# Another written order for the head of a fused memory-attention and spatial-gating kernel

## The chip, the cores and the metric

The kernel runs on one core of a Trainium2 chip. The metric is the device time of one execution in microseconds, the median of several runs. Engines are named as the profile names them: PE is TensorE (PEld its weight loads), DVE VectorE, ACT ScalarE, POOL GpSimd, SP SyncE, which here only issues DMAs.

## What is computed

For each of 8 batches, attention over 32 learned memories in 8 heads, then a gated feed-forward layer that mixes along the sequence:

```python
a = softmax(phi, axis=2)                      # (8, 8, 576, 32)
k_m = einsum('bhsm,bhsd->bhmd', a, k); v_m = einsum('bhsm,bhsd->bhmd', a, v)
attn = softmax(q @ k_m.T / sqrt(64)) @ v_m    # (8, 8, 576, 64)
x = attn.transpose(0, 2, 1, 3).reshape(8, 576, 512)
h = relu(x @ w_in)                            # w_in 512 x 1024
u, v = h[..., :512], h[..., 512:]
v_n = (v - mean(v)) / sqrt(var(v) + 1e-6)
v_s = einsum('ts,bsd->btd', w_spatial, v_n) + b_spatial[None, :, None]
return (u * v_s) @ w_out
```

w_in and w_out arrive as 64-bit floats, so they are decoded on the chip; everything else is 32 bits wide.

## The kernel before

The work is cut into small generator functions; a *step* runs one of them up to its next `yield`, which issues a handful of instructions. There is no scheduler: the order in which steps are taken is the order of the instructions on every engine's queue and on SP's DMA queue, and each engine works through its queue in that order, waiting at an instruction until what it needs is there. The steps of weights and of the first batch (the head) are listed by hand in the string `START`; from the second batch on, `PLAN` gives the order of one batch's steps, taken again for each batch:

```python
for kind, n, ahead in tokens(START):
    step(kind, n, ahead)
for b in range(1, B):
    for at, (kind, n, ahead) in enumerate(steps):
        ...
```

A token is a letter, a block number, a prime for each batch that it works ahead, and `*n` for n steps of it. The letters are:

- P (`memory_weights`): load phi, its maximum over the rows (`mx`, L319 to L325), transposes `mt` and `mb`, the subtraction L349, exp L356, row sums `es`.
- K (`memories`): load k and v, the many small `kvm` matmuls L375 and L387, `den`, then kT and vT.
- Q, S (`queries`, `scores`): q transposed (`tq` by TensorE for the first batch, L478 on VectorE later); scores `sc`, transposed by VectorE (L503), then softmax (maximum L509, subtraction L512, exp L514, sum L517, L519, L520, product L522), transposed back (L533 to L538), split in two parts `ah` (ACT L542) and `al` (DVE L544).
- D, E, L (`load_win`, `decode_win`): w_in's blocks loaded (L178) and decoded: exponent L187, mantissa L193, ACT L205 and L208, DVE L210, the addition L218 (or POOL L216), the product L223 (or POOL L226). X (`prepare_out`) does the same for the four blocks of w_out (`raw_out`, two buffers) and splits each into `woh` and `wol` (L251). The set `ON_VECTOR` says which of the additions, products and splits VectorE does; the rest are GpSimd's.
- W, T, B: load w_spatial and its bias (L260 to L263), transpose it by TensorE (`wt`), split into `wth` and `wtl` (DVE L166 or TensorE L159 with ACT L164); bias row `ws` (POOL L310).
- M (`products`): `mp`, w_in's products with vT, split into `mh` and `ml`.
- V (`gate`): `pv`, relu, statistics (DVE L621, L623), POOL scalars L626 to L631, normalisation on ACT, split into `vh` and `vl` (L641); the fifth block of 64 rows ends in `t` (ACT L645, DVE L649). U (`units`): `pu`, copied to `u` (ACT L672).
- G (`spatial`): `ps`, 28 matmuls per block, the last four with `t` and `ws`; then `g` (L712), `gh` (ACT L723), `gl` (DVE L725). O (`project`): `po` in two halves, the second of which needs blocks 2 and 3 of `gh` and `gl`; then out.

The banks of PSUM are 4 single ones (pool `ps1`) and 2 pairs (`ps2`, for `wt`, `pu` and `ps`).

Of the kernel before, what the change touches and what calls it, by code (L numbers as in the profile page):

```python
# [23 lines left out]


START = """
    P D1 P*3 D0 P*3 D0 P D1 P E0 W L0 E0 D0 E0 T2 L0 P E0 P E0 T2 E0 W P*2 L0 T2*2 P W L0 D0 L1
    L0 E0 T2 E0 L1 W T2*2 L1 K W L1 T4 L1 L0*2 P T1 L1 T4 K L1 T1 Q K D1 T1 D1 T1 K B T1 K T4 K
    Q*2 L0 Q E1 T1 Q P' K Q K Q K E1 L1 T1 Q T4 K E1 K' Q K P' Q P'*2 E1 Q*2 K T0 E1 S E1 P' S T0
    P' T0 S T4 S P' T4 M0 S E1 S T0*3 P' M0*2 X1 P' T0 M0 S*2 P' K' S*2 Q' S*2 T3 E1 T3 P' S P'  # L30
    T3 M0 M1 T3 P'*2 X0 M1 M0 M1 M0 P' M1 Q' M1 S K' S*2 T3 S K' X0 X1 T4 T3 M1 T3 M1 S*2 U1 X1*2
    X0 X1 X0 U0 V1 X0 V1 K' X0 U0 X1 V1 K'*2 X0 V0 U1 Q' K'' P'' V1 V0*2 K' V3 Q' V0 U0 V2 V1 X0
    V1 X1*2 X0 U1 X1 V1 V0 U2 V3 V0 U2 V2 U3 Q' X1 K' U3 K' V4 V3 K' V0 X1 Q' V3 U3 G0 B U2 V4 G1
    V2 K' X0 V4 G0 S'*2 V2 S'*3 G1 V3 M1' P'' X2 M0' P'' X0 V2 V4 V3 V2*2 G1 X3 V4 G0 V4 V3 X2*2
    V4 M0' V4 M1' P'' M1' M0' P'' X2 G1 M0' G1 X2 G0 X3 G2 X2 X3 G2 M1' M0' G0 G1 G0 X2 M0' G2*2
    M1' X2 G1 X3 G3 S' G3 S' P'' X3 G0 G3 X3*2 G0*2 G1*2 P'' G3 G2 S' P'' M1' X2*2 M0' O1 X3 M1'
    X3 G2 G3 O3 S' G3*2 G2 S' G2 X2 X3 O2 K'' O0 S' X3 S' O3 Q'' S' O2 S' G2 S' O3 S'*2 O2 O1 O3
    P''*2 G3 S'*2 P'' O0 O2 P''*2 O1*2 P''*2 G3 O0*2
"""

PLAN = """
# [792 lines left out]
```

## Time and profile before

| | |
|---|---|
| median of 3 runs | 427.18 us (427.04 to 427.68) |
| profiled execution | 425.99 us, of which the span is 424.2 us |
| busy in the span | PE 393.2, PEld 331.6, DVE 299.8, ACT 236.0, POOL 78.9 us |
| granted clock of TensorE | 0.995 on the mean |
| moved by DMA | 50.69 MB |

The span is the time from the first to the last instruction of the profile; the rest of the execution's time lies around it. Busy times of TensorE run from one matmul's start to its modelled end, so pipelined matmuls overlap, and the time from one row's start to the next's is shorter than the duration printed.

### The profile page before, as it was taken

Reading aid. Unit: us, or ns where it says so; the run is one execution under the profiler, and the core shown is the slowest. Engines: PE = TensorE matmul, PEld = TensorE weight load, DVE = VectorE, ACT = ScalarE, POOL = GpSimd, SP = SyncE. Lnnn points to the kernel's source line nnn. Section 1 sums busy time; section 2 is a strip of 40 time slices with the busy share of each in tenths; the row PEclk is TensorE's granted clock in tenths of the full one; section 3 lists DMA queues with packets and bytes.
Section 4 is the critical chain, followed back from the end, with each engine's and each line's share of the span. In section 5 each row is a group of like instructions: output and inputs, shape, how many; then the busy total and the mean of one; then the engine's idle time right before and its main releaser. Section 6 shows DMA issues by size and latency. Waiting matters only on the chain.

```text
span 424.2 us, 9280 instructions
## 1 busy us (share of the span) xinstructions
PE 393.2 (93%) x3828; PEld 331.6 (78%) x3828; DVE 299.8 (71%) x560; ACT 236.0 (56%) x446; POOL 78.9 (19%) x154
## 2 busy tenths in 40 slices
PE   0295998999999999999999999999999999999995
PEld 0172786968988897978888897979798888889884
DVE  1899998995999458955897568946996568834420
ACT  1677787737753376346743575436734476248321
POOL 1345056621200022022200121002100120003100
PEclk9999899999999999999999999999999999999999
DMA  7989935507840948073922659063914500020003
GB/s 287 377 320 289 169 133 181 87 26 132 216 122 16 162 161 181 2 90 109 215 79 55 126 171 168 1 131 109 195 59 69 113 2 2 2 99 2 0 26 99
DMA packets 85790, 50.69 MB, mean 119 GB/s; under 512 B 66226, under 2 KB 70322, under 8 KB 85748
## 3 DMA queue, kind: packets, MB, share of 16 engines
q1 hardware_dynamic: 85748, 50.10, 47.9%
q8 instruction: 30, 0.49, 0.5%
q14 instruction: 12, 0.10, 0.1%
HBM read 40.65 MB, written 9.44 MB: 118 GB/s over the span
## 4 chain that ended last, share of the span: by engine, by line
PE 75%; DVE 13%; DMA 5%; ACT 4%; issue 1%; POOL 1%; SPq 0%; POOLq 0%; DVEq 0%; ACTq 0%
PE ps L701 24%; PE po L741 20%; PE pu L663 11%; PE pv L597 9%; DMA raw<-in_moe_w_in_dram 4%; PE kvm L375 4%; PE mp L565 3%; PE sc L492 2%; DVE power L210 1%; DVE win_sb L218 1%; DVE gl L725 1%; DMA out_dram<-o 1%; DVE st L621 1%; DVE sm L512 1%; PE pv L607 1%
## 5 line engine op out<-in xcount | busy, mean ns | idle before, releaser
L701 PE MATMUL ps<-wth,vh 128*128 128x288 f32 x256 | 57.0, 304 | 0.7 <-ACT u L672 0.4
L626 POOL TENSOR_SCALAR rs<-mv 128x1 f32<-128x1 f32 (+1 forms) x40 | 9.6, 241 | 249.8 <-DVE mv L623 247.2
L723 ACT CAST gh<-g 128x512 fp32r<-128x512 f32 x32 | 19.8, 620 | 63.8 <-DVE g L712 63.8
L701 PE MATMUL ps<-wth,vl 128*128 128x288 f32 x256 | 55.0, 296 | 0.0
L701 PE MATMUL ps<-wtl,vh 128*128 128x288 f32 x256 | 54.5, 294 | 0.0
L741 PE MATMUL po<-woh,gl 128*128 128x512 f32 x128 | 50.9, 398 | 0.8 <-DVE gl L725 0.8
L741 PE MATMUL po<-woh,gh 128*128 128x512 f32 x128 | 50.5, 395 | 0.0
L701 PEld LDWEIGHTS ps<-wth,vh 128*128 128x128 f32 x256 | 41.0, 188 | 12.1 <-ACT mh L574 5.0
L741 PE MATMUL po<-wol,gh 128*128 128x512 f32 x128 | 50.3, 393 | 0.0
L747 ACT COPY o<-po 128x512 f32<-128x512 f32 x36 | 20.9, 586 | 44.1 <-PE po L741 27.5
L701 PEld LDWEIGHTS ps<-wth,vl 128*128 128x128 f32 x256 | 41.0, 188 | 0.3 <-DVE vl L641 0.3
L701 PEld LDWEIGHTS ps<-wtl,vh 128*128 128x128 f32 x256 | 41.0, 188 | 0.0
L636 ACT ACTIVATE vr<-vr,sh,rs 128x512 f32<-128x512 f32 (+1 forms) x40 | 32.6, 814 | 10.2 <-POOL sh L631 9.9
L621 DVE BATCH_NORM_STATS2 st<-vr 128x6 f32<-128x512 f32 (+1 forms) x40 | 27.4, 686 | 12.1 <-ACT vr L602 11.6
L712 DVE TENSOR_TENSOR g<-u,ps 128x576 f32<-128x576 f32 x32 | 23.4, 751 | 12.5 <-PE ps L701 12.5
L741 PEld LDWEIGHTS po<-woh,gl 128*128 128x128 f32 x128 | 24.0, 188 | 8.2 <-DVE gl L725 2.8
L544 DVE TENSOR_TENSOR al<-aT,ah 128x576 fp32r<-128x576 f32 x16 | 12.1, 754 | 24.5 <-ACT ah L542 24.5
L663 PE MATMUL pu<-ah,mh 128*128 128x288 f32 x128 | 28.6, 305 | 0.0
L741 PEld LDWEIGHTS po<-wol,gh 128*128 128x128 f32 x128 | 24.0, 188 | 4.8
L741 PEld LDWEIGHTS po<-woh,gh 128*128 128x128 f32 x128 | 24.1, 188 | 4.6
L663 PE MATMUL pu<-ah,ml 128*128 128x288 f32 x128 | 27.3, 294 | 0.0
L663 PE MATMUL pu<-al,mh 128*128 128x288 f32 x128 | 27.2, 293 | 0.0
(158 smaller groups left out, 893.2 us busy)
## 6 DMA issues: line engine op xcount, KB each, us to landing
kv_sb<-in_k_dram SPq DMA_DIRECT2D x8, 1152.0 KB, 8.1
kv_sb<-in_v_dram SPq DMA_DIRECT2D x8, 1152.0 KB, 9.6
out_dram<-o SPq DMA_DIRECT2D x32, 256.0 KB, 2.4
q_sb<-in_q_dram SPq DMA_DIRECT2D x28, 288.0 KB, 6.2
phi_sb<-in_phi_dram SPq DMA_DIRECT2D x8, 576.0 KB, 4.0
raw<-in_moe_w_in_dram SPq DMA_DIRECT2D x8, 512.0 KB, 7.9
raw_out<-in_moe_w_out_dram SPq DMA_DIRECT2D x4, 512.0 KB, 5.4
w_sb<-in_moe_w_spatial_dram SPq DMA_DIRECT2D x1, 1152.0 KB, 10.8
```

What stands on the lines that cost most here:

```text
L375: nc.tensor.matmul(kvm[r][32 * j : 32 * j + 32], phi_sb[halves[r], j, i, :], kv_sb[halves[r], j, :, i * D : (i + 1) * D], start=(i == 0), ...
L544: nc.vector.tensor_tensor(al[:, r], aT[:, r], ah[:, r, 0:S].bitcast(F32), op=ALU.subtract)
L565: nc.tensor.matmul(mps[r][32 * j : 32 * j + 32, :], vT[D * r : D * r + D, 32 * j : 32 * j + 32], win_sb[D * r : D * r + D, j, cs], start=True,
L597: nc.tensor.matmul(pv, x[:, r, cs], m[:, r, DM:DFF], start=(n == 0), stop=(n == 5))
L621: nc.vector.bn_stats(st6, vr)
L636: nc.scalar.activation(vr, vr, AF.Identity, bias=sh, scale=rs)
L663: nc.tensor.matmul(pu[:, hf, 0:HALF], m[:, r, cs], a[:, r, hf * HALF : (hf + 1) * HALF], start=(n == 0), stop=(n == 5),)
L701: nc.tensor.matmul(ps[:, hf, 0:HALF], a, w[:, hf * HALF : (hf + 1) * HALF], start=(n == 0), stop=(n == len(ops) - 1),)
L712: nc.vector.tensor_tensor(g.rearrange("p (a s) -> p a s", a=2), u[:, dt, :].rearrange("p (a s) -> p a s", a=2), ps[:, :, 0:HALF], op=ALU.mult,
L723: nc.scalar.copy(hi, x)
L741: nc.tensor.matmul(po, a, w, start=(n == 0), stop=(n == 11))
L747: nc.scalar.copy(o, po)
```

## The change

Only the string `START` is another one: the same 382 steps, each kind as often as before, in another sequence. `PLAN`, `ON_VECTOR` and all functions stay. Its first lines, before and after:

```diff
 START = """
-    P D1 P*3 D0 P*3 D0 P D1 P E0 W L0 E0 D0 E0 T2 L0 P E0 P E0 T2 E0 W P*2 L0 T2*2 P W L0 D0 L1
+    P*5 W P D1 P T1 W P*2 D1 P D0 P E0 D0 L0 D0 T2 T1 E0 L0 T1 E0 L0 E0 D0 W T1 L1 K T2 L0 L1 T2
...
 """
```

The order on SP's queue at the start of the program, the loads of phi, w_in (`raw`), w_spatial (`w_sb`, `w_rem`) and its bias (`b_sb`); before:

```order
L330 DMA phi_sb<-in_phi_dram 128x4x288
L178 DMA raw<-in_moe_w_in_dram 128x1024 x4
L260 DMA w_sb<-in_moe_w_spatial_dram 128x4x576
L261 DMA w_rem<-in_moe_w_spatial_dram 64x576
L263 DMA b_sb<-in_moe_b_spatial_dram 1x576 x2
L178 DMA raw<-in_moe_w_in_dram 128x1024 x2
```

and after:

```order
L330 DMA phi_sb<-in_phi_dram 128x4x288
L260 DMA w_sb<-in_moe_w_spatial_dram 128x4x576
L261 DMA w_rem<-in_moe_w_spatial_dram 64x576
L263 DMA b_sb<-in_moe_b_spatial_dram 1x576 x2
L178 DMA raw<-in_moe_w_in_dram 128x1024 x6
```

w_spatial has moved ahead of four loads of w_in; the six loads of w_in now stand together behind it.

On VectorE, from the statistics of the fifth block of V (64 rows) to L649, which gives `t`; before:

```order
L623 BN_AGGR mv<-st_792 64x2
L503 STREAM_TRANSPOSE sm<-sc_0_0_802 128x288
L503 STREAM_TRANSPOSE sm<-sc_0_1_803 128x288
L503 STREAM_TRANSPOSE sm<-sc_1_0_804 128x288
L503 STREAM_TRANSPOSE sm<-sc_1_1_805 128x288
L319 TENSOR_TENSOR half<-phi_sb 128x512
L321 TENSOR_TENSOR half<-half 128x4x64
L641 TENSOR_TENSOR vl<-vr,vh 128x512 x2
L187 TENSOR_SCALAR power<-raw_out 128x512
L193 TENSOR_SCALAR raw_out<-raw_out 128x512
L649 TENSOR_TENSOR t_608<-vr,t_608 64x512
```

and after, with the two transposes that now stand ahead of the statistics:

```order
L187 TENSOR_SCALAR power<-raw_out 128x512
L503 STREAM_TRANSPOSE sm<-sc_0_0_800 128x288
L193 TENSOR_SCALAR raw_out<-raw_out 128x512
L503 STREAM_TRANSPOSE sm<-sc_0_1_801 128x288
L621 BN_STATS st_856<-vr 64x6
L623 BN_AGGR mv<-st_856 64x2
L503 STREAM_TRANSPOSE sm<-sc_1_0_802 128x288
L503 STREAM_TRANSPOSE sm<-sc_1_1_803 128x288
L641 TENSOR_TENSOR vl<-vr,vh 128x512 x2
L509 TENSOR_REDUCE rmx<-sm 128x36
L649 TENSOR_TENSOR t_615<-vr,t_615 64x512
```

The statistics have moved behind two transposes of the scores; L319 and L321 have left this place (L319 now stands further ahead, between the statistics of other blocks, L321 behind), and L509 has come in.

Also on VectorE, further on, where the last `gl` of the first batch and the softmax of the second stand; before:

```order
L712 TENSOR_TENSOR g<-u,ps_2_930 128x576
L166 TENSOR_TENSOR ml<-mp_0_1_857,mh 128x512
L166 TENSOR_TENSOR ml<-mp_1_1_842,mh 128x512
L712 TENSOR_TENSOR g<-u,ps_3_972 128x576
L517 TENSOR_REDUCE rsum<-sm 128x36
L725 TENSOR_TENSOR gl<-g,gh 128x512 x2
L519 TENSOR_SCALAR rsum<-rsum 128x36
L520 RECIPROCAL rsum<-rsum 128x36
L522 TENSOR_TENSOR sm<-sm,rsum 128x1152
L538 STREAM_TRANSPOSE aT<-sm 128x9x32 x2
```

and after:

```order
L166 TENSOR_TENSOR ml<-mp_0_1_874,mh 128x512
L725 TENSOR_TENSOR grl<-g,grh 128x64 x2
L522 TENSOR_TENSOR sm<-sm,rsum 128x1152
L712 TENSOR_TENSOR g<-u,ps_2_934 128x576
L538 STREAM_TRANSPOSE aT<-sm 128x9x32 x2
L712 TENSOR_TENSOR g<-u,ps_3_953 128x576
L725 TENSOR_TENSOR gl<-g,gh 128x512 x2
L544 TENSOR_TENSOR al<-aT,ah 128x576
```

L522 and the first two L538 have moved ahead of the pair of `gl`; L517, L519 and L520 stand earlier still. In the pair, block 3 came first before, and block 2 comes first now; `po` needs block 2 first. GpSimd's order changes at two places: the product for its first w_out block (L226) goes behind the scalars of one more block of V, and L310 goes behind those of the fifth. From the first `pv` of the second batch on, TensorE's order is the same in both.

## Rows read from the trace of the kernel before

**Rows 1.** Stretches: us, busy time of each engine (instructions), granted clock, DMA

```profile
core 0: us, PE busy (x) PEld busy (x) DVE busy (x) ACT busy (x) POOL busy (x), PEclk, DMA share, GB/s
0.00:49.23 49.23, 25.88 (x452) 17.52 (x452) 37.53 (x56) 30.09 (x59) 16.47 (x21) 0.97 0.98 299
49.23:97.02 47.79, 45.24 (x311) 37.48 (x310) 44.90 (x84) 32.88 (x63) 21.66 (x24) 1.00 0.43 112
97.02:424.20 327.18, 322.07 (x3067) 276.65 (x3067) 217.38 (x422) 173.03 (x326) 40.80 (x109) 1.00 0.42 94
```

**Rows 2.** Timeline of PE: start us, us, instruction [idle before <-releaser]

```profile
49.23 0.43 PE L663 MATMUL pu<-ah,mh 128*128 128x288 f32 x2
...
63.00 0.54 PE L701 MATMUL ps<-wth,vh 128*128 128x288 f32 x2 [0.42 <-ACT u L672]
...
73.36 0.79 PE L701 MATMUL ps<-ws,t 128*128 128x288 f32 x4 [1.08 <-DVE t L649]
...
89.97 0.50 PE L741 MATMUL po<-woh,gl 128*128 128x512 f32 x1 [0.85 <-DVE gl L725]
...
97.02 0.50 PE L597 MATMUL pv<-mh,al 128*128 128x512 f32 x1 [0.20 <-DVE al L544]
```

**Rows 3.** Timeline, all engines, 38 to 41 us

```profile
38.24 3.64 POOL L226 TENSOR_TENSOR win_sb<-win_sb,power 128x512 f32<-128x512 f32 x2
38.34 2.40 DVE L512 TENSOR_TENSOR sm<-sm,rmx 128x1152 f32<-128x1152 f32 x1
...
40.66 1.34 DVE L349 TENSOR_TENSOR phi_sb<-phi_sb,mb 128x1152 f32<-128x1152 f32 x1
```

**Rows 4.** Timeline of DVE, 50 to 92 us

```profile
50.99 0.76 DVE L544 TENSOR_TENSOR al<-aT,ah 128x576 fp32r<-128x576 f32 x1 [0.17 <-ACT ah L542]
...
51.80 0.76 DVE L193 TENSOR_SCALAR raw_out<-raw_out 128x512 int32<-128x512 int32 x2
...
53.04 0.69 DVE L621 BATCH_NORM_STATS2 st<-vr 128x6 f32<-128x512 f32 x1
...
58.62 1.67 DVE L223 TENSOR_TENSOR raw_out<-raw_out,power 128x512 f32<-128x512 f32 x1
...
67.99 1.05 DVE L319 TENSOR_TENSOR half<-phi_sb 128x512 f32<-128x512 f32 x1
...
69.42 1.29 DVE L641 TENSOR_TENSOR vl<-vr,vh 128x512 fp32r<-128x512 f32 x2
...
72.62 0.69 DVE L649 TENSOR_TENSOR t<-vr,t 64x512 fp32r<-64x512 f32 x1 [1.24 <-ACT t L645]
...
80.93 1.81 DVE L725 TENSOR_TENSOR gl<-g,gh 128x512 fp32r<-128x512 f32 x1
...
87.52 2.39 DVE L725 TENSOR_TENSOR gl<-g,gh 128x512 fp32r<-128x512 f32 x2
...
90.45 1.36 DVE L522 TENSOR_TENSOR sm<-sm,rsum 128x1152 f32<-128x1152 f32 x1
91.84 0.84 DVE L538 STREAM_TRANSPOSE aT<-sm 128x288 f32<-128x288 f32 x2
```

**Rows 5.** Timeline, waits for the loads of the weights

```profile
10.69 1.29 DVE L187 TENSOR_SCALAR power<-raw 128x1024 int32<-128x1024 int32 x2 [3.18 <-DMA raw<-in_moe_w_in_dram]
...
14.10 1.12 PE L287 MATMUL wt<-ident,w_sb 128*128 128x128 f32 x4 [5.74 <-DMA w_sb<-in_moe_w_spatial_dram]
...
17.32 1.10 DVE L187 TENSOR_SCALAR power<-raw 128x1024 int32<-128x1024 int32 x1 [1.74 <-DMA raw<-in_moe_w_in_dram]
```

**Rows 6.** Chain that ended last: start us, us, what

```profile
45.77 2.95 PE kvm L375 x139
```

**Rows 7.** Timeline of POOL, one of its `wol` splits

```profile
67.18 1.31 POOL L251 TENSOR_TENSOR wol<-raw_out,woh 128x512 fp32r<-128x512 f32 x1
```

**Rows 8.** Stretch of one us, columns as in the first group

```profile
57.00:58.00 1.00, 1.00 (x6) 0.77 (x6) 1.00 (x3) 1.00 (x2) 0.90 (x3) 1.00 0.06 21
```

More of the change, by code (lines that the diff above doesn't have):

```diff
@@ L26 @@
 START = """
-    P D1 P*3 D0 P*3 D0 P D1 P E0 W L0 E0 D0 E0 T2 L0 P E0 P E0 T2 E0 W P*2 L0 T2*2 P W L0 D0 L1
[L28 to L38, printed above, removed]
+    P*5 W P D1 P T1 W P*2 D1 P D0 P E0 D0 L0 D0 T2 T1 E0 L0 T1 E0 L0 E0 D0 W T1 L1 K T2 L0 L1 T2
+    E0 K L1 P L0 L1 P E0 L1 P T2 L0 D1 T1 T2 W T2 E0 W T2 T4 L1 K T4 P L0 T4 K T4 L1 K T4 Q K L1
+    T1 D1 T4 E1 K E1 X0 Q P' Q*2 T1 K Q*5 K Q E1 K E0 K X0 Q P'*2 T3 Q E1 P' K T4 E1 T3 X0 P' S*2
+    B E1 L0 E1 P' T0*2 S P'*2 M0 T0 S*3 P' M0 S E1 T3 T0 M0*2 P' S X1 T3 S M0 M1 S P' T0 S K' X0
+    T3 M1 S M0 M1 T3 K' S T0 P'*2 M0 P' M1 K' P' S*2 K' M1 S T0 Q' S T3 M1*2 K' X1 X0 U2 Q' S*2
+    X1*2 U0 K'*2 V0 K' U0 V1 Q' X1*2 V3 X1 Q' V0 U0 X1 K'' V1 V0 X0 V3 U3 X1 P'' V1 P'' U2 K' X1
+    U3 K' V0*2 V2 V0 V3 X1 V1 Q' V0 V1 K' V3 V4 V1 U2 V1 X0*2 U1 X2 Q' U3 U1 V2 G0 K' V4 X0 V2 G0
+    U1 V2 V3 S' X0 X2 S' X0 V2 G1 X2 G1 S' V3 X2 M1' V4 V2 S' K'' S' V4*4 B M0' V3 V2 M1' S' G0
+    X2 G1 V4 X2 M1' M0' S' G0 X3 G0 M1' G0 G1 M0' Q'' G2*2 G1 X3*2 P'' G3 P''*2 S' X3 G3 X3 M1'*2
+    X2*2 G0 M0' G1 G2 M1' G3 P'' S' X3 X2 G1 X3 S' M0'*2 P'' X2 X3 G1 M0' X3 G1 G0*2 G3 O1 S'
+    X3*2 G2*2 S'*2 G3 G2 O2 P'' S' G2 X2 G3*2 S' O3 S' O0*3 O3 P'' S' O0 S' G3 O2 O3*2 P''*2 O1
+    O2 G2 O1 S' G3 O1 P''*2 G2 P'' O2 P''
 """
```

## Prediction

> **What bounds the kernel now.** I read the stretches first [rows 1]. From 97.02 us to the end TensorE is busy for 322.07 of 327.18 us, and its order there is the same in both kernels: that part is a constant. Between 49.23 and 97.02 us it is busy for 45.24 of 47.79, and before 49.23 for 25.88 of 49.23. So the order of the head can change the time in two ways only: by when TensorE begins its dense stream (the first `pu` matmul, at 49.23), and by the holes behind that. The holes are four [rows 2]: 0.42 us for `u`, 1.08 for `t`, 0.85 for `gl`, 0.20 for `al`, 2.55 in all; three of them wait for VectorE, the first for ScalarE. VectorE itself is busy for 44.90 of the 47.79 us, so in this stretch two engines are nearly full, and a hole on TensorE is VectorE being late.
>
> Why VectorE is late is seen in its rows. At 38.34 the subtraction L512 takes 2.40 us [rows 3] where the like-sized L522 takes 1.36 [rows 4]; GpSimd's product began at 38.24, and two of them took 3.64 us. L349, which reads one operand from a PSUM bank, runs 1.34 us beside the second product [rows 3]. I read this as: an instruction of VectorE with two operands in SBUF and one of GpSimd exclude each other for a whole instruction, and one that reads a bank doesn't take part. The same shows in L223 (1.67 us), L319 (1.05), one `gl` (1.81) and a pair of `gl` (2.39), where a pair of the like `vl` takes 1.29, so 0.65 each [rows 4].
>
> **Up to the first `pu`.** w_spatial is sent ahead of w_in. Its load cost 14.10 - 10.69 = 3.41 us of the queue [rows 5], but the third block of w_in, for which VectorE waits 1.74 us at 17.32 [rows 5], has the same bytes ahead of it in both orders, so it should land at about 17.3 again. What lies earlier moves inside VectorE's empty time: L349 goes to about 10 us, into the 3.18 us wait that ends at 10.69 [rows 5], and the two first L187 wait for their blocks instead (the second until about 10.69 + 3.41 = 14.1). If the third block came later, each us would be paid in full.
>
> From 17.3 on the decode steps of the two orders are the same up to `den`, but one L210 (done before 17.3 until now) stands against one L166. Behind `den` the new order carries one L223 more (it was done), two short steps of w_out (L187, L193), and one L166 less. By the 0.65 and the 0.38 us of such steps at half that length [rows 4] that is 1.3 + 0.76 - 0.65 = 1.4 us, less the short waits for blocks and for ScalarE that it fills; I take VectorE to reach L512 0.2 to 1.0 us later, an estimate. There it costs almost nothing: L512 is held by GpSimd's product at that place now (1.04 us too long), and the chain that starts that product (ScalarE's L208, then two L216) is as late as before within 0.1 us, since L205 goes behind the two L459 and L208 after both. So L512 ends at about 40.9 instead of 38.34 + 2.40 = 40.74. The bounds are 0.7 us earlier (L512 gets in first) and 1 us later (it comes after the product has gone).
>
> Then exp, sums and transposes follow in the same order; ahead of the second `al` (L544, 50.99 [rows 4]) `den` and one L187 stand where two L187 stood, with equal cost. `al` then ends 0.15 us later. On TensorE the `kvm` matmuls that the chain shows from 45.77 for 2.95 us [rows 6] have the same neighbours, and the small stages that are pulled ahead (transposes of w_spatial, `wtl`) lie in time that was idle, at a cost of nothing; without that cover five transposes are the 1.12 us of [rows 5]. `pu` begins at 49.3.
>
> **From there to the last hole.** VectorE starts this part at 51.80 [rows 4] and ends the pair of `gl` at 87.52 + 2.39 = 89.91: 38.11 us. TensorE's third hole ends with it at 89.97. In the new order:
>
> - Moved ahead of the `gl` that is waited for: L519, L520 and L522 (89.91 to 91.84, 1.93) and two L538 (0.84). Gone from the part: one L193, `den` and a short wait (51.80 to 53.04 is 1.24, less half of the 0.76 that stays: 0.86) and one `gl`, since the block that TensorE wants is now the first of the pair (0.65). Sum +1.26.
> - Waits that had their place in the old order: L223 1.02, L319 0.40, `gl` 1.16, the pair 1.10, and the 1.24 before L649 [rows 4]. Sum -4.92.
> - Waits that I expect in their place: GpSimd's product for the first w_out block comes between the two `vl` (one of them held by it, less what it waits itself: 0.65); its last `wol` comes ahead of L522 (1.31, one such instruction alone [rows 7]); 0.15 for the scores, which TensorE does later; and 0.5 before L649. Its answer comes from the fifth block's statistics over GpSimd's scalars and ScalarE; VectorE now makes those statistics later, and with less behind them (two transposes, two `vl` and L509), but without L319 and the rest in between. If the scalars run at once, VectorE doesn't wait there; if a `wol` is again in front of them and the two `vl` hold them, 0.8; I take 0.5. Sum +2.61. From both sides this is 0 (all products beside L166, L712, L503, which read banks, and scalars at once) and 5.5 (two more products ahead of L522 and the pair, 0.8 before L649).
>
> So `gl` ends at 51.95 + 38.11 + 1.26 - 4.92 + 2.61 = 89.01, and TensorE goes on at 89.07 instead of 89.97: -0.90. TensorE by itself would be there at 49.3 + (89.97 - 49.23 - 0.42 - 1.08 - 0.85 = 38.39) = 87.69, so VectorE still sets it. The remaining matmuls up to 97.02 are the same number; `al` is ready about 4 us after `gl`, before they need it, and the 0.20 goes: **-1.10 in all**. L319 of the third batch's phi moves ahead by eleven us, to about 57; the DMA engines have sunk to 21 GB/s by 57 to 58 [rows 8], so that the load has just landed. Were it late, BN, `wol`, `vl` and all behind L319 on VectorE would wait with it.
>
> [...]
>
> The profiled execution took 425.99 us for a span of 424.2; it is 1.19 under the median of the runs shown, 427.18. Taken off both: 424.9 for that execution, **426.1 us** for the median. About 0.2% (0.85 us) is what a measurement of this kernel can tell from no change.
>
> **Rivals.**
> - *Nothing holds VectorE.* GpSimd's products fall beside bank reads throughout. Then TensorE bounds: 87.69 - 89.97 - 0.20 = -2.5, 424.7 us. For it speaks that L166 x2, L712 and L517 stand around the products of w_out now; against it that L522, of two SBUF operands, was moved to where the `wol` run. Chance 0.14.
> - *One more product in front*, or a load that comes 1 us late: +1.31, so +0.2, 427.4 us, no change to be told; half of that is inside it too. The `wol` are two, and both fall due when L522 and the pair do. Chance 0.29.
> - [...] Product and both `wol` each get in ahead of L522, `gl`, `gl`: 2 x 1.31 more than in the sum, -1.10 + 2.62 = +1.5, 428.7 us. It decides from the second one on (at 1.95 us more than the sum has, the end is 0.85 later). For it: the pair was caught this way already (2.39 for 1.29). Against it: L712 and L538 stand between, beside which a `wol` can run. Chance 0.17.
> - The forecast itself has 0.40, and its own range is 425.2 to 426.4.
>
> Faster by over 0.2%: 0.40 + 0.14 = 0.54. Within 0.2%: 0.29. Slower: 0.17. From 424.5 (the first rival and a little) to 428.0 all but the slower case and the ends of the others are inside.
>
> **What would show it.** Right: `pu` begins within 0.4 us of 49.23; a hole of at most 0.5 us before the `ws,t` matmuls; the `gl` that TensorE waits for ends near 89.0, with a hole of 1 to 1.4 us; no wait for `al`. The step at L512 is wrong if it takes 1.4 us. [...] The forecast fails if the w_in blocks land later than 17.3 (then all of it shifts), if L187 of the third w_out block or L319 at 57 us waits for a DMA, or if TensorE finds its banks still held by the scores.

## Result, and the profile after

| | before | after |
|---|---|---|
| median | 427.34 us (427.04 to 427.68, 4 runs) | 422.88 us (422.79 to 423.92, 4 runs) |
| profiled execution | 425.99 us, span 424.2 | 422.92 us, span 421.1 |
| busy in the span | PE 393.2, DVE 299.8, ACT 236.0, POOL 78.9 us | PE 392.9, DVE 295.7, ACT 237.0, POOL 76.7 us |

The ratio of the medians is 0.9907 [0.9885, 0.9930], so the change makes the kernel 4.5 us faster. The forecast was 1.1 us faster, 426.1 us, with a range down to 424.5: too small, and the time lies outside the range. Timed again (the run after_again below) the ratio was 0.9924 [0.9907, 0.9942], 3.5 us.

The stretches of after, cut at the same two instructions as those of before [rows 1]: the first `pu` matmul, and the sixth `pv` matmul of the second batch.

```profile
0.00:48.59 48.59, 25.85 (x451) 16.72 (x452) 37.19 (x57) 30.54 (x59) 16.21 (x21) 1.00 1.01 307
48.59:94.04 45.45, 44.97 (x311) 37.73 (x310) 42.35 (x87) 34.44 (x64) 19.70 (x24) 1.00 0.41 113
94.04:421.10 327.06, 322.09 (x3068) 276.52 (x3066) 216.20 (x420) 171.98 (x323) 40.80 (x109) 1.00 0.41 94
```

The profiled executions differ by 3.1 us: 49.23 - 48.59 = 0.64 up to the first `pu`, 47.79 - 45.45 = 2.34 in the middle, and 0.12 in the long rest. The medians differ by more. The profiled execution of before was one of its faster ones (425.99 against a median of 427.34); a second profile of the same kernel (before_again below) begins `pu` 1.06 us later.

Of the four holes of TensorE [rows 2] one is left, that for `u`; and before the `po` matmul that had waited 0.85 us for `gl` less than 0.1 us is empty. TensorE's rows there, from 61 and from 87 us:

```profile
61.12 0.54 PE L663 MATMUL pu<-ah,mh 128*128 128x288 f32 x2 [0.43 <-ACT u L672]
...
87.26 0.39 PE L741 MATMUL po<-wol,gh 128*128 128x512 f32 x1
87.57 0.19 PEld L741 LDWEIGHTS po<-woh,gl 128*128 128x128 f32 x1 [0.36 <-DVE gl L725]
87.58 0.51 PE L741 MATMUL po<-woh,gl 128*128 128x512 f32 x1
```

The weight load still ends its wait with `gl`, but the matmul begins 0.32 us after the one ahead of it, where the others follow each other at 0.23. VectorE and TensorE meet here with nothing to spare on either side.

VectorE from the start of this part to `al`, the rows that answer to [rows 4]:

```profile
51.56 0.42 DVE L193 TENSOR_SCALAR raw_out<-raw_out 128x512 int32<-128x512 int32 x1
...
55.24 0.66 DVE L223 TENSOR_TENSOR raw_out<-raw_out,power 128x512 f32<-128x512 f32 x1
...
56.64 0.66 DVE L319 TENSOR_TENSOR half<-phi_sb 128x512 f32<-128x512 f32 x1
...
60.55 0.69 DVE L641 TENSOR_TENSOR vl<-vr,vh 128x512 fp32r<-128x512 f32 x1 [0.53 <-ACT vh L639]
...
65.34 0.48 DVE L503 STREAM_TRANSPOSE sm<-sc 128x288 f32<-128x288 f32 x1 [0.44 <-PE sc L492]
...
71.06 0.69 DVE L649 TENSOR_TENSOR t<-vr,t 64x512 fp32r<-64x512 f32 x1 [0.40 <-ACT t L645]
...
83.18 1.35 DVE L522 TENSOR_TENSOR sm<-sm,rsum 128x1152 f32<-128x1152 f32 x1
...
86.50 1.62 DVE L725 TENSOR_TENSOR gl<-g,gh 128x512 fp32r<-128x512 f32 x2
88.05 0.75 DVE L544 TENSOR_TENSOR al<-aT,ah 128x576 fp32r<-128x576 f32 x1
```

And GpSimd's products in the same part:

```profile
62.53 1.30 POOL L226 TENSOR_TENSOR raw_out<-raw_out,power 128x512 f32<-128x512 f32 x1 [2.32 <-DVE raw_out L218]
...
66.38 1.32 POOL L251 TENSOR_TENSOR wol<-raw_out,woh 128x512 fp32r<-128x512 f32 x1
...
83.81 3.16 POOL L251 TENSOR_TENSOR wol<-raw_out,woh 128x512 fp32r<-128x512 f32 x2 [0.77 <-ACT woh L249]
```

L223 and L319 take 0.66 us each now. The product at 62.53 runs beside a transpose and L617, the `wol` at 66.38 beside the statistics (BN) and transposes, and at 83.18 L522 is in first: 1.35 us for it, while two `wol` take 3.16 instead of the 1.31 each of [rows 7]. Of the last two `wol` and the pair of `gl`, the shortest, median and longest duration in ns, and the first and last start:

```profile
L251 POOL TENSOR_TENSOR wol<-raw_out,woh x2: 1317/1602/1888, 83.8 to 85.7; 128x512 fp32r<-128x512 f32 x2
L725 DVE TENSOR_TENSOR gl<-g,gh x2: 682/852/1021, 86.5 to 87.4; 128x512 fp32r<-128x512 f32 x2
```

So GpSimd pays most: the first `wol` takes 1.89 us. VectorE still pays a little: the first `gl`, the one that TensorE waits for, begins beside the second `wol` and takes 1.02 us instead of 0.68.

Up to the first `pu`, the rows that answer to [rows 5] and [rows 3]:

```profile
10.01 1.35 DVE L349 TENSOR_TENSOR phi_sb<-phi_sb,mb 128x1152 f32<-128x1152 f32 x1 [2.48 <-PE mb L347]
11.31 0.69 DVE L187 TENSOR_SCALAR power<-raw 128x1024 int32<-128x1024 int32 x1
13.80 0.72 DVE L187 TENSOR_SCALAR power<-raw 128x1024 int32<-128x1024 int32 x1 [1.80 <-DMA raw<-in_moe_w_in_dram]
...
17.05 0.68 DVE L187 TENSOR_SCALAR power<-raw 128x1024 int32<-128x1024 int32 x1
...
38.36 2.11 DVE L512 TENSOR_TENSOR sm<-sm,rmx 128x1152 f32<-128x1152 f32 x1
```

What differs most in TensorE's rows is the second batch's `kvm`. Of the tile's rows, with the shortest, median and longest duration in ns, first before, then after:

```profile
L375 PE MATMUL kvm<-kv_sb,phi_sb x144: 269/298/419, 45.7 to 48.5; 64*32 64x128 f32 x144
```

```profile
L375 PE MATMUL kvm<-kv_sb,phi_sb x144: 269/269/293, 45.0 to 47.0; 64*32 64x128 f32 x144
```

In before, part of them take 0.42 us instead of 0.27. The granted clock of both kernels there (us, busy time of each engine, clock, DMA):

```profile
44.00:46.00 2.00, 1.76 (x18) 0.82 (x26) 1.97 (x4) 1.60 (x4) 0.00 (x0) 0.52 0.95 248
46.00:48.00 2.00, 2.00 (x104) 2.00 (x96) 1.90 (x8) 1.65 (x5) 0.00 (x0) 0.62 1.48 146
```

```profile
44.00:46.00 2.00, 1.55 (x74) 1.47 (x82) 1.97 (x4) 1.47 (x3) 0.00 (x0) 1.00 1.63 135
46.00:48.00 2.00, 1.26 (x92) 0.99 (x78) 1.90 (x7) 1.39 (x4) 0.00 (x0) 1.00 0.88 69
```

Before, TensorE's granted clock is 0.52 and 0.62 from 44 to 48 us, behind an empty stretch of 2.59 us that ends at 42.46; after, it stays at 1.00, and TensorE's longest empty stretch between 34 and 46 us is 1.32 us.

The group is 0.86 us shorter by that (2.25 instead of 3.11), but `pu` is not earlier by as much, since the small matmuls with `es` stand between, and VectorE makes `es`. Before, then after:

```profile
47.95 0.29 DVE L325 TENSOR_TENSOR es<-es,phi_sb 128x128 f32<-128x128 f32 x1
48.55 0.30 PE L387 MATMUL kvm<-ones,es 64*32 64x2 f32 x16
```

```profile
47.71 0.29 DVE L325 TENSOR_TENSOR es<-es,phi_sb 128x128 f32<-128x128 f32 x1
48.05 0.27 PE L387 MATMUL kvm<-ones,es 64*32 64x2 f32 x16 [0.79 <-DVE es L325]
```

Before, `es` is there at 48.24 and TensorE comes later; after, TensorE stands for 0.79 us until it is there. By these rows the 0.64 us part, by an estimate, into three: 0.26 for the clock (with matmuls that followed `es` at once, at 48.29, before would have begun `pu` at 48.97), 0.24 because `es` is earlier, and 0.14 because one `wt` matmul that stood between these and `pu` now stands ahead of `kvm`. `es` is earlier because L512, which begins at 38.36 against 38.34, is held for less: GpSimd's product begins 0.26 us earlier.

```profile
37.98 3.63 POOL L226 TENSOR_TENSOR win_sb<-win_sb,power 128x512 f32<-128x512 f32 x2
```

### The profile page after: what moved, and what is told of

Read it like the earlier page. It is cut to its first block, busy times and chain, and to the rows that moved or that the text cites. A ratio compares the mean times of both kernels' runs of the same rounds, so it can differ in the third digit from the quotient of the medians.

```text
span 421.1 us, 9279 instructions
## 1 busy us (share of the span) xinstructions
PE 392.9 (93%) x3828; PEld 331.0 (79%) x3828; DVE 295.7 (70%) x560; ACT 237.0 (56%) x446; POOL 76.7 (18%) x154
## 4 chain that ended last, share of the span: by engine, by line
PE 83%; DVE 7%; ACT 3%; DMA 3%; issue 2%; POOL 1%; POOLq 0%; SPq 0%; DVEq 0%; ACTq 0%
PE ps L701 28%; PE po L741 23%; PE pu L663 11%; PE pv L597 9%; PE kvm L375 4%; PE mp L565 3%; PE sc L492 2%; DMA w_sb<-in_moe_w_spatial_dram 2%; DMA out_dram<-o 1%; ACT raw L208 1%; PE pv L607 1%; PE pv L606 1%; PE wt L287 1%; DVE phi_sb L349 1%; DVE win_sb L223 1%
```

## The experiments

All were timed in alternation with the kernel before on one chip per group; the ratio is to that. "First pu" is the start of the first `pu` matmul in the profiled execution, and "from there" the rest of its span. The two columns part what happens ahead of TensorE's dense stream from what happens behind.

| label | median us (range) | ratio to before | first pu | from there |
|---|---|---|---|---|
| before_again | 426.77 (425.94 to 427.67) | 1.0002 [0.9988, 1.0017] | 50.29 | 374.5 |
| early_new | 426.00 (425.49 to 430.04) | 0.9998 [0.9979, 1.0017] | 51.01 | 374.8 |
| late_new | 425.22 (424.46 to 426.31) | 0.9966 [0.9953, 0.9979] | 49.78 | 372.9 |
| before_warm | 431.61 (430.09 to 433.31) | 1.0117 [1.0091, 1.0143] | 51.78 | 378.0 |
| after_again | 423.24 (422.95 to 425.07) | 0.9924 [0.9907, 0.9942] | 48.69 | 372.5 |
| w_only | 429.51 (428.11 to 430.06) | 1.0055 [1.0039, 1.0072] | 51.59 | 375.2 |
| pair_swap | 424.07 (423.56 to 426.36) | 0.9943 [0.9923, 0.9962] | 48.65 | 373.5 |
| product_early | 428.71 (425.51 to 430.07) | 1.0028 [1.0004, 1.0051] | 50.48 | 376.4 |
| soft_back | 424.14 (423.79 to 425.65) | 0.9941 [0.9922, 0.9960] | 49.02 | 373.1 |
| after_robust | 424.74 (422.58 to 428.34) | 0.9948 [0.9924, 0.9971] | 50.32 | 372.2 |
| product_robust | 428.18 (425.74 to 431.06) | 1.0033 [1.0011, 1.0054] | 50.77 | 376.3 |
| after_hold | 424.12 (422.06 to 426.32) | 0.9939 [0.9920, 0.9959] | 51.21 | 372.6 |
| product_hold | 428.33 (424.86 to 429.75) | 1.0033 [1.0012, 1.0054] | 50.14 | 376.4 |
| after_warm | 426.47 (425.38 to 427.63) | 0.9983 [0.9970, 0.9996] | 50.51 | 373.1 |
| product_warm | 430.56 (428.79 to 432.00) | 1.0084 [1.0058, 1.0110] | 50.81 | 378.3 |
| better | 423.84 (422.23 to 426.12) | 0.9931 [0.9907, 0.9956] | 49.91 | 372.2 |
| better_hold | 425.14 (424.56 to 425.57) | 0.9960 [0.9945, 0.9976] | 51.09 | 372.3 |
| better_warm | 425.88 (425.03 to 426.62) | 0.9976 [0.9964, 0.9988] | 50.12 | 373.9 |

For kernels with the same order behind `pu` and no added matmuls the last column moves by at most 0.7 us; for those with the changed order up to `pu` the one before it lies between 48.6 and 51.0 us. That is what the later groups are about.

### Which half does it

before_again is the kernel before itself. The other two join the two orders at the first step of U (`pu`): early_new takes the new order up to there and then what is left of the old, late_new the reverse.

```diff
--- before
+++ early_new
-    P D1 P*3 D0 P*3 D0 P D1 P E0 W L0 E0 D0 E0 T2 L0 P E0 P E0 T2 E0 W P*2 L0 T2*2 P W L0 D0 L1
...
+    P*5 W P D1 P T1 W P*2 D1 P D0 P E0 D0 L0 D0 T2 T1 E0 L0 T1 E0 L0 E0 D0 W T1 L1 K T2 L0 L1 T2
...
     V2 K' X0 V4 G0 S'*2 V2 S'*3 G1 V3 M1' P'' X2 M0' P'' X0 V2 V4 V3 V2*2 G1 X3 V4 G0 V4 V3 X2*2
...
```

```diff
--- before
+++ late_new
     P D1 P*3 D0 P*3 D0 P D1 P E0 W L0 E0 D0 E0 T2 L0 P E0 P E0 T2 E0 W P*2 L0 T2*2 P W L0 D0 L1
...
-    X0 X1 X0 U0 V1 X0 V1 K' X0 U0 X1 V1 K'*2 X0 V0 U1 Q' K'' P'' V1 V0*2 K' V3 Q' V0 U0 V2 V1 X0
...
+    X0*2 K' X0 U2 X1*2 U0 K'*2 V0 K' U0 V1 Q' X1*2 V3 X1 Q' V0 U0 X1 K'' V1 V0 X0 V3 U3 X1 P''
...
```

> The kernel before once more, for a second profile of it. Its profiled execution took 425.99 us and its timed runs 427.04 to 427.68, so the profile that the prediction was worked from may be a lucky one. Clock theory: a usual execution, of about 427.3 us and a span of about 425.5, shows TensorE at the lower of its two clock levels for longer than the 44 to 47.5 us of the first profile, so that the kvm matmuls and the first pu and pv take over a us longer; the holes stay at about 2.5 us. Rival: the clock is the same and the 1.3 us are waits elsewhere (a later block of w_in, or wider holes behind VectorE).

> The new order up to the first pu matmul, the old order for what is left of the head. Theory of two parts: the first pu comes at 48.6 us as in the new kernel and the kvm matmuls run in 2.2 us; the holes for u, t, gl and al stay (2.0 to 2.6 us), so 425.0 to 426.3 us, that is 1.0 to 2.3 less than before, the larger the more the clock costs in usual executions of before. Rival, VectorE's lead alone closes the holes: 423 us as the new kernel.

> The old order up to the first pu matmul, the new order for what is left of the head. Theory of two parts: pu begins where it does before (49.2 us in the profile), and the holes shrink from 2.55 to about 0.5 us, VectorE losing no time to GpSimd's products at L223, L319 and two gl: 2.0 to 2.4 us less than before, 425.0 us. Rival, the holes close only because of what is done early: less than 0.8 us gained, 426.5 to 427.4.

before_again gave the same median, but its profile starts `pu` at 50.29, 1.06 us later than the first profile of the same kernel. 0.41 us of that is there already when its empty stretch ends (42.87 instead of 42.46); the rest comes behind it, with the clock at 0.50 for all of 42 to 48 us. late_new is worth about 1.5 to 1.7 us in the medians and 1.6 to 2.1 from the first `pu` on; of its holes only that for `u` stays, and has grown to 1.56. early_new keeps all four holes of before. Its profiled execution starts `pu` late, at 51.01; seven of its twelve times lie between 425.5 and 426.0, about 1 us under before's median, and the others above. So the late half is worth some 1.5 us by itself. The early half by itself shows no gain that is clear of noise (0.9998), though most of its times are lower. Both together give 3.5 to 4.5 us, which is more than the two apart.

### The late half: gl, softmax, GpSimd's product

pair_swap puts the pair of `gl` back in the old order, soft_back the softmax of the second batch (L522 and what follows) behind that pair, and product_early moves three steps of the first w_out block ahead, so that GpSimd makes its product ahead of the scalars of V. The diffs show pieces of `START`. Theories A, B and C are those of the expectations.

```diff
--- after
+++ pair_swap
-    S'*2 G3 G2 O2 P'' S' G2 X2 G3*2 S'
+    S'*2 G3 G2 O2 P'' S' X2 G3*2 G2 S'
--- after
+++ soft_back
-    S' X3*2 G2*2 S'*2 G3 G2 O2 P'' S' G2 X2 G3*2 S'
+    X3*2 G2*2 G3 G2 O2 P'' G2 X2 G3*2 S'*5
--- after
+++ product_early
-    X0 V3 U3 X1 P'' V1 P''
+    X0 V3 U3 X0*3 X1 P'' V1 P''
...
-    V1 X0*2 U1 X2
+    V1 U1 X2
...
-    V4 X0 V2
+    V4 V2
```

> The changed kernel with the pair of gl in the old order, block 3 ahead of block 2, nothing else. Theory A (VectorE ends the gl of block 2 with no slack, 0.1 us before TensorE's matmul needs it): block 3 must wait for its gh, ends near 88.0, and block 2's gl near 88.6 instead of 87.4; a hole of 1.0 to 1.3 us before that po matmul, and 1.0 to 1.2 us more in all (ratio to the kernel before 0.0025 higher than that of after_again). Theory B (TensorE by itself sets the pace there and has room): hole at most 0.3 us, time the same within 0.3 us.

> The changed kernel with the softmax of the second batch put back behind the pair of gl (L522, the first two L538 and the copy ah behind them), block 2 still ahead of block 3. Theory A (TensorE's own work sets the pace behind t, and VectorE ends gl just in time, so 2.2 us less work ahead of gl can give no more than the 0.1 us that is left there; al is then ready near 92.3 us and needed at 93.3): same within 0.2 us. Theory B (moving the softmax ahead cost time, as the forecast's sum had it): 0.5 us or more faster. Theory C (moving it ahead is what closed the hole before the pv matmul that needs al): a hole of 0.3 to 1 us there and as much slower.

> The changed kernel with three steps of the first w_out block (L210, the addition L218, GpSimd's product L226) put back directly ahead of VectorE's L223 of the second block, so that GpSimd makes this product before the scalars of the first block of V and beside L223. Theory A (it is GpSimd's placement that closed the hole before the matmuls with t): L223 or the instruction next to it is held, 1.6 to 2.0 us instead of 0.66; the scalars and with them normalisation come 1.5 to 2.5 us later; a hole of 0.8 to 2 us before the ps matmuls or those with ws and t; 1 to 2 us more in all. Theory B (the holes closed because of the other moves, the softmax pulled ahead and L319 spread): time within 0.4 us of after_again.

pair_swap opened a hole of 0.98 us before the `po` matmul and cost 0.83 us against after_again in the medians (the intervals of the two ratios overlap) and 0.94 from the first `pu` on: theory A, a little under its 1.0. VectorE ends `gl` with almost no slack, so its place in the pair is worth nearly what it takes.

soft_back cost 0.7 us by the ratios (their intervals overlap), and 0.6 from the first `pu` on, which is theory C's size but not its place. The rows of soft_back from the pair of `gl` to the hole:

```profile
84.23 3.04 POOL L251 TENSOR_TENSOR wol<-raw_out,woh 128x512 fp32r<-128x512 f32 x2 [0.77 <-ACT woh L249]
...
85.08 2.73 DVE L725 TENSOR_TENSOR gl<-g,gh 128x512 fp32r<-128x512 f32 x2
...
87.74 1.34 DVE L522 TENSOR_TENSOR sm<-sm,rsum 128x1152 f32<-128x1152 f32 x1
...
89.99 0.67 ACT L542 CAST ah<-aT 128x576 fp32r<-128x576 f32 x1 [4.22 <-DVE aT L538]
90.57 0.58 ACT L747 COPY o<-po 128x512 f32<-128x512 f32 x1
...
91.20 0.33 PE L347 MATMUL mb<-ident,cmb 128*128 128x128 f32 x1 [0.77 <-ACT o L747]
```

Without L522 there, the two `wol` meet the pair of `gl` and it takes 2.73 us instead of 1.62. `gl` is in time all the same; the softmax behind is later, ScalarE stands at `ah` for 4.22 us with the copy of `o` queued behind it, and TensorE's next small matmul waits for the bank which that copy frees. So moving the softmax ahead did two things, and the run does not part them: the long L522 is in before GpSimd's last `wol`, and ScalarE's queue doesn't stand. The hole comes from the second.

product_early showed the price of GpSimd's place, larger than expected. Its rows:

```profile
58.47 1.68 POOL L226 TENSOR_TENSOR raw_out<-raw_out,power 128x512 f32<-128x512 f32 x1 [17.33 <-DVE raw_out L218]
...
60.23 0.56 POOL L626 TENSOR_SCALAR rs<-mv 128x1 f32<-128x1 f32 x1
...
61.84 0.82 ACT L636 ACTIVATE vr<-vr,sh,rs 128x512 f32<-128x512 f32 x1 [2.13 <-POOL sh L631]
...
65.63 0.85 PE L663 MATMUL pu<-ah,mh 128*128 128x288 f32 x2 [3.04 <-ACT u L672]
```

L223 is in first this time and is not held (0.69 us). What costs is the queue: the scalars wait behind the product, which itself waits for L218, although their own operand is there at 57.22; ScalarE's normalisation comes behind the scalars (11.4 us after the first `pu` instead of 8.9), and the copy of `u` behind that, for 3.04 us on TensorE instead of 0.43. That is 2.6 of the 3.9 us that this kernel takes longer from `pu` on (376.4 against 372.5). Behind the empty stretch the granted clock is 0.50 from 66 to 68 us; that this is the other 1.3 us fits, but isn't shown. Theory A was right that GpSimd's place is what counts; it named the wrong victim, and the cost is about twice what it said.

### The early half: w_spatial, the clock, and the executions that lose it

w_only moves w_spatial's loads alone; before_warm puts 16 matmuls of the identity, with results that nothing uses, into TensorE's empty stretch near 40 us of the kernel before; after_again is the changed kernel once more.

```diff
--- before
+++ w_only
-    P D1 P*3 D0 P*3 D0 P D1 P E0 W L0 E0 D0
+    P W D1 P*3 D0 P*3 D0 P D1 P E0 L0 E0 D0
--- before
+++ before_warm
-    S*2 Q' S*2 T3 E1 T3 P' S P'
+    S*2 Q' S*2 T3 Z*4 E1 T3 P' S P'
```

> The kernel before with one step moved: the loads of w_spatial and its bias go directly behind phi's, everything else as before. Theory A (the forecast's step: it costs nothing and gives nothing alone, since the third w_in block has the same bytes ahead of it): second L187 waits until about 14 us, third L187 at 17.3 to 17.9, first pu within 0.4 us of that of the kernel before, ratio 0.998 to 1.002. Theory B (the load's place is what brought the earlier pu): pu 0.6 us or more earlier, ratio 0.9985 or less. Theory C (the decode of the first blocks now comes too late): pu 0.5 us later or more, ratio above 1.001.

> The kernel before with four steps of four more 128x128 matmuls each, of the identity with itself into a bank that nobody reads, on TensorE in the wait between 39.9 and 42.5 us. Nothing else moves. Clock theory: the clock doesn't fall at 44 us, kvm takes 2.2 us in place of 2.95, pu begins at about 48.9 (then al bounds it), and usual executions lose what they have above the first profile: 425.6 to 426.4 us. Rival, the clock there costs nothing since al bounds the first pu anyway: 427.0 to 427.7 us.

> The changed kernel once more, unchanged, timed against the kernel before on one chip. Theory A (the early gain belongs to the order): first pu at 48.4 to 49.0 us, TensorE's granted clock at 1.00 from 36 to 54 us, L319 of the second phi at 32.0 us without a wait for its load, 422.9 us on the median (422.4 to 423.4), ratio 0.990. Theory B (the early part of the new order is decided by when that load lands, from execution to execution, as early_new showed: load 0.9 us late, L210 held by the product, clock at 0.50, pu at 51.0): a median near 425, or times in two groups 2 us apart.

w_only was 0.55% slower. Its row where VectorE begins to decode w_in:

```profile
13.89 1.29 DVE L187 TENSOR_SCALAR power<-raw 128x1024 int32<-128x1024 int32 x2 [6.25 <-DMA raw<-in_moe_w_in_dram]
```

Four steps and L349 stand behind that in the old order, so that L512 is 2.2 us later than in before_again (40.92 against 38.74). The load's new place gains nothing by itself; that it is free in the changed kernel fits the rows there, where L349, one L187 and the transposes of w_spatial fill the time ahead of what is late.

before_warm kept the clock at 1.00 from 36 to 52 us, and the second `kvm` took 2.30 us instead of the 2.84 of before_again: the clock is what makes that group long. But TensorE then stood for 2.09 us at 51 and 1.94 at 112 us with nothing in the profile that it waited for, and the kernel was 1.2% slower.

after_again gave theory A: `pu` at 48.69, clock 1.00 from 36 to 54 us, 423.24 us. Of the ten times of the changed kernel in the two groups, eight lie between 422.8 and 423.7, and two at 423.9 and 425.1, with mean clocks of 0.990 and 0.987. In product_early, with the same steps up to `pu`, nine of twelve times lie 1.5 us or more above the other three. What goes with a late `pu` is seen beside early_new, which shares these steps as well. First early_new:

```profile
32.92 0.69 DVE L319 TENSOR_TENSOR half<-phi_sb 128x512 f32<-128x512 f32 x1 [0.88 <-DMA phi_sb<-in_phi_dram]
...
35.17 3.51 POOL L216 TENSOR_TENSOR win_sb<-win_sb,raw 128x512 f32<-128x512 f32 x2 [7.03 <-ACT raw L208]
35.32 2.23 DVE L210 SCALAR_TENSOR_TENSOR power<-raw,power 128x1024 int32<-128x1024 int32 x1
```

In after_again L319 runs at 32.12, L210 begins at 34.52, ahead of GpSimd's L216 at 34.91, and takes 1.18 us. In early_new phi lands 0.8 us later, L210 comes 0.15 us behind L216 and takes 2.23; TensorE waits 1.66 us for what is behind it, and its clock is 0.50 from 38 to 44 us. Three pairs of kernels were to take that apart. _robust moves L210 ahead, _hold L325 and L210, _warm adds 20 matmuls of the identity ahead of the first `kvm` (unused results). A Z step is four such matmuls.

```diff
--- after, product_early
+++ after_robust, product_robust
-    T4 E1 T3 X0 P' S*2 B E1
+    T4 E1*2 T3 X0 P' S*2 B
--- after, product_early
+++ after_hold, product_hold
-    T4 E1 T3 X0 P' S*2 B E1
+    T4 E1 P' E1 X0 T3 S*2 B
--- after, product_early
+++ after_warm, product_warm
-    T1 T2 W T2 E0 W T2
+    T1 T2 W Z*5 T2 E0 W T2
```

> The changed kernel with one step moved: VectorE's L210 of the last w_in block stands directly behind L323 of the second phi, so 1.1 us further ahead (before L193, L325 and the first transpose of the scores). Theory A (the slow executions of the new order are those in which the load of the second phi lands 0.5 to 0.9 us later, L210 then starts behind GpSimd's additions L216 at 35.0 us and is held a whole instruction, 2.2 us instead of 1.2): L210 at 33.5 to 34.4 us, never held; no execution above 424 us; median 423.0 to 423.3; first pu at 48.6 to 48.9. Theory B (the slow executions come from something else, such as the clock falling by itself): one in six or more still 1.5 us above the others.

> The kernel product_early with the same one step moved (L210 of the last w_in block 1.1 us further ahead). product_early fell into two groups, 425.5 to 425.6 us (3 of 12) and 427.2 to 430.1 (9 of 12). Theory A (the two groups are L210 ahead of GpSimd's L216 or behind it): now nearly all at 425.4 to 426.0, median 425.6, clock 1.00 from 36 to 54 us, L210 at 1.2 us; what is left over the changed kernel, 2.5 us, is the price of GpSimd's early product alone. Theory B (the lower clock comes on its own): median still above 428.

> The changed kernel with L325 of the second phi and VectorE's L210 of the last w_in block both directly behind L323, so that no instruction of VectorE with two SBUF operands is left to start after about 34.7 us, where GpSimd's additions L216 begin (34.9 to 35.2). Theory A (the slow executions are an instruction of this kind behind L216: L210 in early_new and product_early, L325 in after_robust): none held, even where phi lands 0.9 us late; first pu at 48.6 to 49.5 in the profile, no execution above 424.5 us, median 423.0 to 423.4. Theory B (the low clock in some executions has its own cause, not a held instruction): clock below 0.99 in one of six or more, these 1.5 us or more above the rest.

> product_early with the same two instructions moved. Theory A: the group at 427 to 430 us, 9 of 12 in product_early, is gone or nearly so, and the median is at 425.5 to 426.2; what stays over the changed kernel is the hole of 3.0 us before the pu that waits for ScalarE's u, 2.6 us more than there. Theory B: median still above 427.5 with a clock of 0.98 to 0.99.

> The changed kernel with 20 matmuls of the identity (their results unused) in TensorE's empty time between 15.4 and 20.7 us, ahead of the first group of kvm. In the profiles so far 144 kvm matmuls of the first batch take 0.417 us each at first and 0.269 later, the turn coming at another place in each execution (the group lasts 3.15 to 4.09 us), and the load of the second phi is issued when they end (26.0 to 27.1 us), since it goes into the same buffer. Theory A (this is where the slow executions start: a late turn, a late phi, then VectorE's instruction behind GpSimd's L216 and the low clock at 36 to 42 us): kvm in 2.3 to 2.6 us, phi's load issued near 25.2 and no wait at L319, no slow executions, median 422.4 to 423.0. Theory B (as in before_warm, the added instructions make TensorE wait for nothing that the profile shows): holes put down to issue of 1 us or more, and the time 1 to 3 us longer than the changed kernel's.

> product_early with the same 20 matmuls. Theory A: the group at 427 to 430 us (9 of 12 there) is gone, median 425.4 to 425.8. Theory B: median above 427.5, from the late phi or from waits for instructions.

All six missed their theory A in the time. In after_robust L210 is not held, but L325, now behind it, takes 1.37 us instead of 0.29. In after_hold neither is, but the next one:

```profile
35.09 2.90 POOL L216 TENSOR_TENSOR win_sb<-win_sb,raw 128x512 f32<-128x512 f32 x2 [7.02 <-ACT raw L208]
35.34 1.51 DVE L193 TENSOR_SCALAR raw_out<-raw_out 128x512 int32<-128x512 int32 x1
```

L193 has one tensor operand and takes 0.42 us in after_again (33.59). And in product_hold nothing was held, yet `pu` began at 50.14: with L210 ahead, TensorE stands for 1.27 us before the `mt` transpose, and the clock was 0.50 from 36 to 42 us all the same. So a late `pu` doesn't need a held instruction. What makes the clock fall isn't shown: an empty stretch of 1.22 us that ends at 33.96 in before, and the one of 1.32 us that ends at 41.67 in after, left it at 1.00. Nor is the clock all: in after_robust and after_hold TensorE waits 0.79 us for `es` ahead of `pu`, as in after, so there it is VectorE that is late, and how much of that comes from the held instruction and how much from the slower TensorE wasn't parted.

after_warm was built on an earlier link. In all profiles of the new order the load of the second phi is issued when the first `kvm` has ended, since it goes into the same buffer; without added matmuls that end lies between 25.8 and 26.9 us. The rows of that first group in early_new and in after_warm:

```profile
L375 PE MATMUL kvm<-kv_sb,phi_sb x144: 417/417/418, 22.8 to 26.5; 64*32 64x128 f32 x144
```

```profile
L375 PE MATMUL kvm<-kv_sb,phi_sb x144: 269/269/294, 23.2 to 25.2; 64*32 64x128 f32 x144
```

With TensorE busy ahead of it, the group is short: that link is shown. Then phi is there without a wait, nothing is held near 35 us, and the clock is 1.00 from 36 to 54. But TensorE also stood for 2.17 us up to 29.38 without a cause in the profile, and for 1.46 at 105; behind the first stop the `tq` rows near 33 us take 0.42 us each and those from 33.50 on 0.27, and GpSimd's L216 came at 37.75, 2.6 us later than in after and behind L210 (36.26) in any case. And an early issue didn't always bring phi early: soft_back issues the load at 26.20 and waits 0.65 us for it, after at 26.78 and doesn't wait. The time is no better, and where the late executions start stays open.

### A version that is faster than both?

better moves the copy of `u` ahead of the second `vh`, and L210 of the first w_out block between the two `vl`, on top of after_robust; better_hold and better_warm do the same on the other two.

```diff
-    V1 U2 V1 X0*2
+    U2 V1 X0 V1 X0
```

> after_robust with two more steps moved: ScalarE's copy of u (L672) ahead of the second vh copy, so that the last hole of TensorE at 61.2 us (0.43) goes, and VectorE's L210 of the first w_out block between the two vl, into the 0.53 us that VectorE waits there. Theory A (that hole is on the path and VectorE is as full as TensorE): the hole goes, VectorE gains up to 0.4 of its wait, and 0.2 to 0.45 us less than after_robust, if gl keeps up. Theory B (VectorE's gl has no slack at all): the hole before the po matmul of block 2 grows by as much, time the same within 0.1 us. Theory C: a vl held by GpSimd's product, 0.5 us or more slower.

> The kernel better with the same two instructions moved (u's copy ahead of the second vh copy, L210 of the first w_out block between the two vl). Theory A: the times of better that were over 423.5 us go; median 422.3 to 422.8, 0.3 to 0.6 us below after_hold, since the hole of 0.43 us for u falls to about 0.2. Theory B: the same median as after_hold.

> The changed kernel with the same 20 matmuls, and with u's copy ahead of the second vh copy and L210 of the first w_out block between the two vl. Theory A: 0.2 to 0.4 us less than after_warm, the hole for u at 0.2 us or less. Theory B: no difference, the 0.2 us hole before the matmuls with t grows instead.

The hole for `u` fell from 0.43 to 0.16 us (better), and 0.20 for `t` came. From the first `pu` to the `po` matmul that takes `gl`, the three take 31.93, 31.89 and 31.74 us, and the kernels that they were built on 32.06, 32.01 and 31.88: a gain of 0.12 to 0.14, under theory A's 0.2. The medians don't show it: against the kernel that it was built on, better is 0.9 us lower, better_hold 1.0 higher and better_warm 0.6 lower. The lowest time of all was after_hold's 422.06; no version has a lower median than the changed kernel (422.88, and 423.24 in after_again).

## Why the prediction was wrong

- **The sum missed by 2.00 us, -1.10 against -3.10 in the spans.** Along its own steps that is 0.39 at the start of VectorE's part, 0.90 in the waits of the new place, 0.20 in all other terms of VectorE's part, 0.39 behind the `po` matmul with `gl`, and 0.12 behind the sixth `pv`.
- **The step that failed most: the waits in the new place, 2.61 us.** That two engines are nearly level was right, and VectorE still comes last, though by 0.1 us and not by 1.4; this term was too large. Measured are 0.53 + 0.44 + 0.40 = 1.37 us of empty time, and 0.34 for the `gl` that a `wol` holds: 1.71. Of the two waits for GpSimd in it (0.65 and 1.31) only this 0.34 came: the product ran beside a transpose and a bank read, and L522 was in before the `wol`. With 1.71 and the real start of 51.56 the same sum gives 87.72, and the `gl` ended at 87.52; so the other terms held within 0.2 us in their total (they were not measured one by one).
- **The step at L512, an end at about 40.9: off by 0.43.** It ended at 40.47. L512 was to begin 0.2 to 1.0 us later and began as before, and GpSimd's product, said to be as late as before within 0.1 us, began 0.26 us earlier. VectorE's part therefore begins at 51.56 and not at 51.95.
- **`pu` begins at 49.3: wrong.** It began at 48.59 and 48.69. The step said that the second `kvm` has the same neighbours, and took its 2.95 us over. The group takes 2.25 us at a granted clock of 1.00, and then TensorE waits for `es`. The small stages of TensorE that the change spreads were costed at nothing, as cover; with them no empty stretch there is longer than 1.32 us, and the clock stayed at 1.00, though no run shows that this is the reason. In the two profiles of before it falls, each time at another point, and `pu` starts at 49.23 and at 50.29 us.
- **The 0.20 for `al`: too small.** From the `po` matmul with `gl` to the sixth `pv` TensorE took 7.05 us before and 6.46 after, 0.59 less. The idle time printed counts from the modelled end of the matmul ahead; from start to start the matmul with `al` came 0.60 us behind the one ahead of it (96.42 and 97.02), where the others follow at 0.23.
- **The rival "nothing holds VectorE" is nearly what happened** in this part, with 0.34 us for one `gl`. It had a chance of 0.14 and 424.7 us for the median, still above the 422.88 measured. TensorE by itself would have been at `gl` at 48.59 + 38.39 + 0.43 = 87.41, the 0.43 being the hole for `u`, which the forecast had as closed; it went on at 87.58. The remark that "L522, of two SBUF operands, was moved to where the `wol` run" was weighed as a danger; soft_back, with the pair of `gl` at 2.73 us, speaks for its being a protection.
- **The working from one profile to the median** took this execution's `pu` for the usual one. That goes with 3.1 us in the spans becoming 3.5 to 4.5 in the medians; with two profiles of before it is not measured further.
- **w_spatial ahead of w_in costs nothing: right for the whole** (third L187 at 17.05 without a wait, L349 at 10.01, second L187 at 13.80, as worked out), wrong if it stood alone: w_only. The 1.12 us that the forecast gives for five transposes is a row of four; nothing rests on it.
- **Right besides:** no wait for `al` (88.05 and 91.58, needed at 93.34 and later), no hole before `ws,t`, L319 of the third phi at 56.64 without a wait. The hole of 1 to 1.4 us for `gl` was forecast, and is below 0.1.
- **The other rivals** did not happen. One more product in front was not tried as such: in product_early the product came earlier, did not hold VectorE, and cost 2.6 us through GpSimd's own queue: the scalars, ScalarE and the copy of `u`.

## What to carry to other kernels

When two engines are nearly level, as here, work out both ends and give the case "the other engine sets it" the chance that its margin deserves; a list of possible collisions is not a list of collisions until the rows of each engine's queue say who is in first. Behind an empty stretch of 2.59 us the granted clock of before was 0.52 from 44 to 46 us, and behind one of 1.32 us in after it was 1.00, so look at the granted clock on both sides of each hole before taking a duration over, and then at what the engine would wait for next: a group that is 0.86 us shorter gained an estimated 0.26 here. With matmuls added as a filler the clock was 1.00 near 40 us (36 to 52 us in before_warm, 36 to 54 in after_warm), but before_warm, after_warm and product_warm were each slower than the same kernel without them, so they are no remedy here. And when the time of one kernel scatters by two us, take a second profile before costing a change of one.

## What the runs showed of the hardware that was not expected

- A VectorE instruction with one tensor operand was held by GpSimd too: L193 took 1.51 us beside L216 (after_hold; 1.50 in better_hold) and 0.42 in after_again. The forecast's reading, two operands in SBUF, was too narrow. L517, a reduction, was not held: 1.34 us beside L216 in after, and 1.35 at 41.70 with GpSimd empty:

```profile
79.05 1.34 DVE L517 TENSOR_REDUCE rsum<-sm 128x36 f32<-128x1152 f32 x1
79.05 1.32 POOL L216 TENSOR_TENSOR raw_out<-raw_out 128x512 f32<-128x512 f32 x1
```

- The first `kvm` ran its matmuls at 0.417 us, as long as the longest of the second `kvm` of before (0.419), where the granted clock was 0.50 (45 to 47 us); but here, at 22 to 27 us, the records give a clock of 1.00. Where they turned to 0.269, it was at another point in each execution, and in early_new, product_early and after_robust none of the group did. It took 2.74 (w_only) to 4.09 us where no matmuls were added.
- With twenty matmuls more in an idle stretch TensorE stopped later for 2.02 to 2.88 us near 29 us and for 1.46 to 1.62 near 105 to 111 (three kernels), with sixteen for 2.09 and 1.94 us (before_warm), with nothing in the profile that it waited for. No run here shows the cause.
